# Which queue carries the third and fourth block of x at the start of a one-core kernel

## The chip, the cores and the metric

The kernel runs on one core of one Trainium2 chip. Times are device microseconds of one execution. Before the change three runs were timed: 234.91 us is their median, 234.7 and 235.87 us the ends. A separate execution was recorded by the hardware profiler; all rows of the profile come from that one.

## The reference

The input A_q (2048 tokens, 640 wide, bf16) is normalised per token; the result xn feeds two branches, and both are added to A_q. Cut to what matters:

```python
x = A_q
xn = _layernorm(x, axis=-1)
# branch A: a 4-tap shift of k, times v, a causal convolution of length 2048 per channel
# (by Fourier transforms), plus kv * ssm_D, times xn
# branch B:
g = jnp.einsum("bsd,df->bsf", xn, w_gate)          # 640 -> 1728
u = jnp.einsum("bsd,df->bsf", xn, w_up)
h = _sigmoid(g) * u
B = jnp.einsum("bsf,fd->bsd", h, w_down)           # 1728 -> 640
return x + A + B
```

## The kernel before, in words

The 2048 tokens lie as 16 blocks: token 16 p + b is partition p of block b, so one block is a tile of 128 x 640, 160 KB, whose rows are 1280 bytes each. Four blocks make a token tile t of 512 tokens. Branch B runs tile by tile: for each of 14 chunks of 128 hidden columns a gate product and an up product of five matmuls each (the 640 channels are five chunks of 128), the sigmoid on ScalarE (L300), the product of both on VectorE (L306), then the down products. Branch A works on five chunks of 128 channels, with matmuls against Fourier tables, evictions by ScalarE and VectorE, and round trips through DRAM. The long middle of the kernel is a list of steps whose order over all engines is written out by hand (ORDER); each engine works its own instructions in that order. Nearly all transfers are issued from SyncE, in the order of that list; SyncE's queue is q1 in the profile, ScalarE's is q10. 

The change is at the front, ahead of the list, where the first token tile is got ready block by block:

- x blocks 0 and 1 are loaded in halves of 320 columns, one half from SyncE and one from ScalarE (L515).
- x blocks 2 and 3 are loaded whole (L517), one from each queue.
- Gate and up columns 0 to 255 (load_w, L184 and L187; 320 KB each, in rows of 512 bytes) follow on SyncE, then columns 256 to 511, then the transfers of the list.
- For each block, VectorE takes the statistics (bn_stats, L213, two per block; L217, L241), GpSimd the power -1/2 (L245), and VectorE writes the normalised block xn (L250). On VectorE these stand in the order: statistics of 0, statistics of 1, xn of 0, statistics of 2, xn of 1, statistics of 3, xn of 2, xn of 3, with the small steps between.
- TensorE turns each xn block by five transposes (turn, L264), ScalarE copies the result to xnT (L267).
- TensorE then works the string FIRST: gate and up products of the first two hidden chunks in quarters of 128 tokens (quarter, L282), "g01" being gate, chunk 0, block 1, and "t2" the turn of block 2:

```python
FIRST = """
g00 g10 t1 u00 u10 t2 g01 g11 u01 u11 t3 g02 u02 g12 u12 g03 u03 g13 u13
"""
```

Block 0 is turned before that. Ahead of the real products TensorE runs matmuls on zeros (busy, L528). ScalarE's first work is one small activation with its table load (L130).

Of the kernel before, what the change touches and what calls it, by code (L numbers as in the profile page):

```python
# [65 lines left out]
def kernel(  # L66
# [14 lines left out]
    nc = tc.nc  # L81
    xr = A_q.flatten_outer_dims().rearrange("(p b) d -> p b d", b=NB)
# [33 lines left out]
    x = res.tile([P, NB, DM], BF16, name="x")  # L116
# [15 lines left out]
    sync = nc.sync  # L132
# [381 lines left out]
        for i in range(2):  # L514
            (sync, nc.scalar)[i].dma_start(x[:, b, 320 * i:320 * i + 320], xr[:, b, 320 * i:320 * i + 320])  # L515
    for i in range(2):
        (sync, nc.scalar)[i].dma_start(x[:, 2 + i, :], xr[:, 2 + i, :])  # L517
    for u in range(2):
        load_w(sync, 0, 256, u)
    for u in range(2):  # L520
# [210 lines left out]
```

## Time and profile before

| what | value |
|---|---|
| three timed runs | 234.7, 234.91, 235.87 us |
| the profiled execution | 235.94 us |
| its span, first to last instruction | 234.2 us |
| TensorE busy | 227.0 us, 97% of the span |
| VectorE busy | 204.1 us, 87% |
| ScalarE busy | 131.5 us, 56% |
| DMA q1 (SyncE) | 55.35 MB, 88.2% of 16 engines |
| DMA q10 (ScalarE) | 0.36 MB, 0.5% |
| granted TensorE clock | full throughout |

Times in the rows are microseconds from the start of the span. A row of the timeline has the start, the duration, the engine (SPq and ACTq are the queues' issues by SyncE and ScalarE, PEld the weight loads of TensorE), the line, the operation, what is written and read, the number of instructions and, in brackets, the idle time before it and what ended it. The duration of an issue is the time that it takes to hand the transfer over, not the time of the transfer. DMA engines' busy share can be over 1 where packets overlap.

### The profile page before, as it was taken

The numbers are of one execution on the slowest core, as the hardware profiler recorded it, in microseconds if no ns is written. First come the engines' busy times: TensorE is split into PE (matmuls) and PEld (weight loads), VectorE is DVE, ScalarE is ACT, GpSimd is POOL, SyncE is SP. The second block draws the span as 40 slices with busy tenths as digits, with TensorE's granted clock in tenths as the row PEclk, the third lists the DMA queues.
The fourth block names the chain that finished last, engine by engine and source line by source line (L and its number), as shares of the span: only waits on it lengthen the run. The fifth ranks groups of instructions, "written<-read, shape, count | busy, mean of one in ns | idle before, by whom it ended". The sixth has DMA issues, their size and how long they took to land.

```text
span 234.2 us, 5584 instructions
## 1 busy us (share of the span) xinstructions
PE 227.0 (97%) x2270; PEld 112.8 (48%) x2281; DVE 204.1 (87%) x323; ACT 131.5 (56%) x191; POOL 12.7 (5%) x27
## 2 busy tenths in 40 slices
PE   7799999999999999999999999999999999999993
PEld 2664444447444444446444444445563545445582
DVE  5532789999969999999999999999999999999574
ACT  2347832438985877866647666855555776652000
POOL 5201200000020000012001000000000000000000
PEclk9999999999999999999999999999999999999999
DMA  6999999799789987978879998999989769784775
GB/s 176 278 305 235 246 344 203 208 243 304 198 270 293 317 213 211 249 164 243 212 261 266 309 272 214 271 227 258 321 200 247 213 180 255 182 217 145 216 266 148
DMA packets 98143, 56.07 MB, mean 239 GB/s; under 512 B 56326, under 2 KB 92358, under 8 KB 97990
## 3 DMA queue, kind: packets, MB, share of 16 engines
q1 hardware_dynamic: 97542, 55.35, 88.2%
q10 hardware_dynamic: 576, 0.36, 0.5%
q8 instruction: 18, 0.29, 0.5%
q14 instruction: 7, 0.06, 0.1%
HBM read 35.39 MB, written 18.35 MB: 229 GB/s over the span
## 4 chain that ended last, share of the span: by engine, by line
PE 79%; DVE 12%; DMA 4%; issue 2%; SPq 1%; ACT 1%; DVEq 0%
PE pg L291 22%; PE pu L291 22%; PE pd L329 14%; PE psb L500 3%; PE pr L340 3%; PE ps L400 3%; PE ps L398 3%; DMA w<-in_B_w_up_dram 3%; PE ps L432 3%; PE psa L461 2%; DVE tmp L377 2%; PE pg L312 1%; DVE acc L379 1%; DVE yx L505 1%; DMA SMt<-tabSM 1%
## 5 line engine op out<-in xcount | busy, mean ns | idle before, releaser
L291 PEld LDWEIGHTS <-w 128*128 128x128 bf16 x500 | 47.1, 98 | 57.4 <-issue 4.0
L291 PE MATMUL pu<-xnT,w 128*128 128x512 bf16 x250 | 62.2, 379 | 0.0
L291 PE MATMUL pg<-xnT,w 128*128 128x512 bf16 x250 | 62.2, 379 | 0.0
L329 PE MATMUL pd<-wd,hT 128*128 128x512 bf16 x213 | 50.4, 379 | 0.7 <-issue 0.2
L306 DVE TENSOR_TENSOR hT<-sig,pu 128x512 bf16<-128x512 bf16 x52 | 34.6, 679 | 12.8 <-ACT sig L300 6.9
L254 ACT CAST t<-ps 128x1024 bf16<-128x1024 f32 x33 | 32.3, 1013 | 21.9 <-PE ps L400 21.9
L300 ACT ACTIVATE sig<-pg 128x512 bf16<-128x512 f32 x52 | 30.6, 598 | 23.7 <-PE pg L291 20.1
L254 ACT CAST xz<-ps 128x1024 bf16<-128x1024 f32 x30 | 29.5, 1015 | 14.3 <-PE ps L432 14.3
L329 PEld LDWEIGHTS <-hT 128*128 128x128 bf16 x224 | 21.3, 98 | 25.1 <-issue 0.9
L447 DVE TENSOR_TENSOR xz<-xz 128x2048 bf16<-128x2048 bf16 x20 | 24.4, 1218 | 0.3
L377 DVE TENSOR_TENSOR tmp<-kx,sc 128x1024 bf16<-128x1024 bf16 x30 | 20.9, 698 | 0.4
L379 DVE TENSOR_TENSOR acc<-acc,tmp 128x1024 bf16<-128x1024 bf16 x30 | 20.6, 685 | 0.5
L505 DVE TENSOR_TENSOR yx<-psb,xn 128x512 bf16<-128x512 f32 x20 | 13.8, 688 | 2.6 <-PE psb L500 1.8
L400 PE MATMUL ps<-kvh,S1t 128*128 128x512 bf16 x40 | 15.5, 387 | 0.0
L254 ACT CAST ao<-psa 128x1024 bf16<-128x1024 f32 x11 | 10.8, 1014 | 8.3 <-PE psa L461 8.2
L398 PE MATMUL ps<-kvh,S1t 128*128 128x512 bf16 x40 | 15.1, 379 | 0.0
L445 DVE STREAM_SHUFFLE xz<-xz 128x512 f32<-128x512 f32 x20 | 14.5, 725 | 0.0
L340 PE MATMUL pr<-wd,hT 128*128 128x128 bf16 x224 | 13.8, 219 | 0.0
L340 PEld LDWEIGHTS <-hT 128*128 128x128 bf16 x224 | 13.0, 98 | 1.8 <-issue 0.6
L334 DVE TENSOR_TENSOR x<-pd,x 128x512 bf16<-128x512 f32 x16 | 10.7, 684 | 2.1 <-PE pd L329 2.0
L257 DVE CAST xz<-ps 128x1024 bf16<-128x1024 f32 x10 | 12.1, 1215 | 0.4 <-PE ps L432 0.4
L500 PEld LDWEIGHTS <-TBt 128*128 128x128 bf16 x160 | 9.7, 98 | 3.4 <-issue 1.5
(57 smaller groups left out, 183.9 us busy)
## 6 DMA issues: line engine op xcount, KB each, us to landing
d<-t SPq DMA_DIRECT2D x20, 512.0 KB, 5.1
t<-d SPq DMA_DIRECT2D x20, 512.0 KB, 5.5
bi<-d SPq DMA_DIRECT2D x8, 512.0 KB, 5.3
d<-ao SPq DMA_DIRECT2D x6, 512.0 KB, 5.7
kvh<-in_A_v_dram SPq DMA_DIRECT2D x10, 256.0 KB, 5.3
kx<-in_A_k_dram SPq DMA_DIRECT2D x10, 256.0 KB, 4.6
hn<-in_A_ssm_k_dram SPq DMA_DIRECT2D x20, 128.0 KB, 4.6
x<-in_A_q_dram SPq DMA_DIRECT2D x3, 640.0 KB, 5.1
```

Source lines behind the costliest of these rows:

```text
L254: nc.scalar.copy(out=out, in_=in_)
L291: nc.tensor.matmul(pg[:, :], lhsT=w[:, c, u * UP + fc * P:u * UP + (fc + 1) * P], rhs=xnT[:, :, c, :], start=(c == 0), stop=(c == NC - 1))
L300: nc.scalar.activation(sig[fc][:, :], pgs[0, fc][:, :], ACT.Sigmoid)
L306: nc.vector.tensor_tensor(hT[:, fc, :], sig[fc][:, :], pgs[1, fc][:, :], ALU.mult)
L329: nc.tensor.matmul(pds[bb][:, :], lhsT=hT[:, fc, bb * P:(bb + 1) * P], rhs=wd[:, fc, 0:4 * P], start=(fc == 0), stop=(fc == NFC - 1))
L340: nc.tensor.matmul(pds[t, b0][:, bb, :], lhsT=hT[:, fc, bb * P:(bb + 1) * P], rhs=wd[:, fc, 4 * P:DM], start=(fc == 0), stop=(fc == NFC - 1))
L377: nc.vector.tensor_tensor(d["tmp"][:, :, :], kx[:, lo + 3 - m:hi + 3 - m, :], sb(m), ALU.mult)
L379: nc.vector.tensor_tensor(d["acc"][:, :, :], d["acc"][:, :, :], d["tmp"][:, :, :], ALU.add)
L398: nc.tensor.matmul(ps[:, 0, :, :], lhsT=S1[:, h, :], rhs=cin[c]["kvh"][:, 0, 4 * n4:4 * n4 + 4, :], start=True, stop=True)
L400: nc.tensor.matmul(ps[:, 1, :, :], lhsT=S1[:, h, :], rhs=hp[:, 2 * n4:2 * n4 + 2, :, :], start=True, stop=True)
L447: nc.vector.tensor_tensor(z[:, 1:3, :, :], z[:, 0:1, :, :].to_broadcast((P, 2, 8, P)), z[:, 1:3, :, :], ALU.mult)
L500: nc.tensor.matmul(ps[:, i, :], lhsT=TB[:, h, 4 * m + i, :], rhs=bi[:, h, 4 * (m % 2) + i, :], start=(h == 0), stop=(h == 1))
```

## The change

Both whole blocks of x are issued from ScalarE, block 2 first and block 3 behind it, after ScalarE's halves of blocks 0 and 1. SyncE's queue thereby holds its halves of blocks 0 and 1 and directly behind them the first gate and up columns. The number, size and program order of the transfers stay the same.

```diff
     for i in range(2):
-        (sync, nc.scalar)[i].dma_start(x[:, 2 + i, :], xr[:, 2 + i, :])
+        nc.scalar.dma_start(x[:, 2 + i, :], xr[:, 2 + i, :])
     for u in range(2):
         load_w(sync, 0, 256, u)
     for u in range(2):
         load_w(sync, 256, 512, u)
```

## The prediction

> **What bounds the kernel now.** I read the page's busy times first, then the table of engine busy time by stretch, then the chain of waits for the first 14 us, and last the timeline and the DMA view of those microseconds. The table by stretch tells where lost time can be:
>
> ```profile
> core 0: us, PE busy (x) PEld busy (x) DVE busy (x) ACT busy (x) POOL busy (x), PEclk, DMA share, GB/s
> 0.00:8.10 8.10, 5.61 (x18) 1.95 (x18) 5.01 (x17) 2.18 (x3) 4.02 (x14) 1.00 0.77 210
> 9.30:36.00 26.70, 26.70 (x184) 14.52 (x185) 13.84 (x21) 15.20 (x31) 2.64 (x5) 1.00 1.06 279
> 90.00:120.00 30.00, 29.63 (x295) 14.59 (x296) 29.49 (x45) 21.63 (x32) 2.96 (x3) 1.00 0.88 223
> ```
>
> From 9.3 us on, TensorE is busy for all of 26.70 us, and even in the stretch where VectorE is fullest (29.49 of 30.00 us) it loses 0.37 us. So the time at which TensorE's real work gets going decides the end, and a change at the front is worth at most the shift of that point. The chain says what sets the point:
>
> ```profile
> 1.65 0.42 SPq L517
> 2.07 0.04 issue
> 2.12 0.43 SPq L184
> 2.55 0.04 issue
> 2.59 6.63 DMA w<-in_B_w_up_dram
> 9.22 0.05 issue
> 9.27 0.73 PE pu L282 x10
> ```
>
> The chain goes through SyncE's issue of x block 2 (L517), the first gate columns (L184) and the first up columns, waits 6.63 us until those up columns have landed at 9.22 us, and continues on TensorE. The edit takes the L517 link of 0.42 us out of exactly this chain, so it looks like a gain. The question is whether 6.63 us is counted from the issue (then all of it moves) or ends when the bytes ahead have gone through (then nothing moves).
>
> **Part 1: SyncE's queue loses one issue.** The issues as they stand:
>
> ```profile
> 1.16 1.28 ACT L130 ACT_TABLE_LOAD   x1 [1.16 <-PEq L715]
> 1.65 0.42 SPq L517 DMA_DIRECT2D x<-in_A_q_dram  x1
> 1.65 0.45 ACTq L517 DMA_DIRECT2D x<-in_A_q_dram  x1
> 2.12 0.43 SPq L184 DMA_DIRECT2D w<-in_B_w_gate_dram  x1
> 2.59 0.53 SPq L187 DMA_DIRECT2D w<-in_B_w_up_dram  x1
> 3.22 0.94 SPq L184 DMA_DIRECT2D w<-in_B_w_gate_dram  x1
> 4.20 1.50 SPq L187 DMA_DIRECT2D w<-in_B_w_up_dram  x1
> 5.74 3.03 SPq L184 DMA_DIRECT2D w<-in_B_w_gate_dram  x2
> ```
>
> Without block 2 the gate columns are issued at 1.65 instead of 2.12 us: 0.47 us earlier, and the up columns as well. The transfers behind them gain less: the third and fourth weight transfers take 0.94 and 1.50 us to issue, and the next two 3.03 us together, where a free issue takes 0.43 us. From 3.22 us on SyncE is held up by transfers that are still queued, so its head start runs out there; nothing later comes sooner by it unless the engines have moved more by then. Whether they have is read from the transfer side:
>
> ```profile
> 2.00:3.00 1.00, 1.00 (x4) 0.44 (x3) 0.01 (x1) 0.65 (x2) 1.00 (x3) 1.00 0.97 285
> 3.00:4.00 1.00, 1.00 (x4) 0.32 (x3) 0.97 (x3) 0.00 (x0) 0.04 (x1) 1.00 0.88 166
> 4.00:5.00 1.00, 1.00 (x4) 0.30 (x2) 0.96 (x4) 0.00 (x0) 0.53 (x1) 1.00 0.85 287
> 5.00:6.00 1.00, 1.00 (x8) 0.43 (x7) 0.79 (x4) 0.00 (x0) 0.13 (x2) 1.00 1.07 320
> 6.00:7.00 1.00, 0.79 (x6) 0.18 (x3) 0.94 (x3) 0.69 (x1) 0.47 (x1) 1.00 1.12 306
> ```
>
> The last two columns are the DMA engines' busy share and rate, one row for each microsecond. From 2 us on the 16 engines are never empty: 0.97, 0.88, 0.85, then over 1. All that must land before the up products is the same before and after: four blocks of x and two weight transfers, 4 x 160 + 2 x 320 = 1280 KB, in another order. An earlier issue can only fill what is unfilled: 0.03 + 0.12 + 0.15 = 0.30 us of the three first rows. That is the upper end of the ordinary gain. I take 0, because the unfilled part is in the rows after 3 us, when weights issued at 2.12 and 2.59 us stood in the queue already: the engines were slow there, not short of work. The row 3 to 4 us is the odd one, 166 GB/s at 88% busy; it comes back as a rival.
>
> **Part 2: ScalarE's queue gains one issue.** Block 3 is issued behind block 2, at 1.65 + 0.45 + 0.05 = 2.15 instead of 1.65 us, and one more issue of 0.45 us stands on ScalarE. Behind it is only the warm-up activation; the table load (1.16 us, 1.28 us long) already runs beside the issue at 1.65 us, and ScalarE's first product copy is far behind:
>
> ```profile
> 6.18 0.69 ACT L267 COPY xnT<-pt 128x640 bf16<-128x640 bf16 x1 [3.52 <-PE pt L264]
> ```
>
> It had been idle for 3.52 us. Cost 0; if that cover were gone it would be 0.45 us.
>
> **Part 3: when blocks 2 and 3 land.** Which queue gets how much of the engines is seen where both hold work. The two queues' rows for 2 to 3 us (both hold 640-byte rows of x), and after them for 5.5 to 6 us:
>
> ```profile
> q1 hardware_dynamic: 258, 0.15, 51.1%
> q10 hardware_dynamic: 236, 0.14, 45.6%
> ...
> q1 hardware_dynamic: 315, 0.16, 106.3%
> q10 hardware_dynamic: 3, 0.00, 1.5%
> ```
>
> q1 is SyncE's, q10 ScalarE's: 258 packets against 236, turn by turn. In 5.5 to 6 us ScalarE's queue starts its last three, so block 3 ends there, about when block 2 does. Now each of block 2's 128 rows takes its turn with one 512-byte weight row instead of a 1280-byte row of block 3: 128 x 768 = 98 KB less ahead of its end, 0.3 us at 306 GB/s. Block 3 follows, with 256 weight rows let through before its end: 131 KB, 0.43 us later. Who waits for them:
>
> ```profile
> 5.67 0.15 DVE L241 TENSOR_SCALAR lnq<-mv 128x1 f32<-128x1 f32 x1
> 6.05 0.89 DVE L213 BATCH_NORM_STATS2 st<-x 128x6 f32<-128x320 bf16 x2 [0.23 <-DMA x<-in_A_q_dram]
> 7.51 0.88 DVE L213 BATCH_NORM_STATS2 st<-x 128x6 f32<-128x320 bf16 x2
> 8.30 0.43 DVE L250 TENSOR_SCALAR xn<-x,mv,lnq 128x640 bf16<-128x640 bf16 x1
> 9.71 0.45 DVE L250 TENSOR_SCALAR xn<-x,mv,lnq 128x640 bf16<-128x640 bf16 x1 [0.67 <-POOL lnq L245]
> 8.13 0.73 PE L282 MATMUL pg<-xnT,w 128*128 128x128 bf16 x10 [1.34 <-DMA w<-in_B_w_gate_dram]
> 9.78 0.32 PEld L264 LDWEIGHTS <-xn 128*128 128x128 bf16 x5
> 11.18 0.32 PEld L264 LDWEIGHTS <-xn 128*128 128x128 bf16 x5
> ```
>
> The statistics of block 2 waited 0.23 us for it, until 6.05 us; this wait goes, and VectorE is free at 5.82. Block 3's statistics start at 7.51 us without a wait, or 7.28 once the 0.23 are gone. Block 3 then lands some 0.43 us after its old end, near 6.5 to 6.8 us: still in time. And what is gained here ends in slack: xn of block 2 is ready at 8.30 + 0.43 = 8.73 and its turning starts at 9.78 (1.05 us later); xn of block 3 is ready at 10.16 and turned at 11.18 (1.02 us later). TensorE reaches these turns only after the weight waits, so neither a small gain nor a small loss in x moves the end.
>
> **Sum.** 0 (part 1, bounds -0.30 and 0) + 0 (part 2) + 0 (part 3). Against the profiled execution, 235.94 us with a span of 234.2, that is 235.9; its 1.74 us outside the span are untouched. That execution lay 1.03 us above the median of the three timed runs (234.91; 234.7 to 235.87), so the forecast for the median is **234.9 us**, and 0.5%, about what a measurement of this kernel can tell from no change, is 1.17 us.
>
> At part 3 one rule speaks against the change. The Trainium skill, page "DMA: Bandwidth & Descriptors", section "Queues, rings and completion order", says that a DMA engine takes a whole packet from one queue, typically 9 to 17 descriptors and up to 64, before it turns to the other. With 64 weight rows for each engine ahead of block 2, 64 x 16 x 512 bytes = 524 KB, block 2 would, as an estimate from that page and the 306 GB/s, land 1.7 us later, at 7.76; by the slack above that adds 7.76 - 7.07 = 0.7 us, 235.6 instead of 234.9. The trace cannot show it: where two queues met, both carried x.
>
> **The rivals.**
>
> *A. ScalarE's queue gets the smaller share (slower).* Now the long weight transfers compete with x from the first moment, where they came behind half of it. Block 2's statistics stand at the head of VectorE's line; behind them are xn of block 1 and everything of blocks 2 and 3. The deciding point is block 2 landing at 6.05 + 1.02 = 7.07 us; every microsecond beyond is one on the end. If it lands only with the gate columns (TensorE's start at 8.13) the price is 1.06 us: 236.0. If only with the up columns (9.22) it is 2.15 us: 237.1. For it: 512-byte weight rows stand in long lines of 640 KB against 320 KB of x. Against it: the 258 to 236 above. Chance 0.19.
>
> *B. The slow microsecond goes, or the laggard catches up (faster).* In 3 to 4 us, just when 1280-byte rows of x went through both queues, the rate was 166 instead of 287 GB/s. If it is that pairing, the edit ends it: (287 - 166) / 287 = 0.42 us earlier, 234.5. And the transfers are uneven over the engines; for 0 to 9.2 us the DMA view has
>
> ```profile
> q1 hardware_dynamic: 3110, 1.67, 68.2%
> ```
>
> SyncE's queue owed 0.98 MB by then (320 KB of x, 640 KB of weights); it had moved 1.67, so 0.69 MB of later transfers, some two of them, were through before the last part of the up columns. At 9.22 - 8.13 = 1.1 us for a transfer, an even spread would bring the up columns some 2 us sooner, of which the turns' slack lets 1.02 + 0.23 = 1.25 us through: 233.7. For it: nothing but that the order at the very spot changes. Against it: no row ties the lag to the order, and the three timed runs already differ by 1.2 us. Chance 0.23 in all, 0.15 of it near the end of 233.7 or below.
>
> *C. The change does not do what it says.* SyncE's issue could be held at the second weight transfer already, so the weights' order hardly moves. No time changes: 234.9. Chance 0.06; the forecast itself has 0.52.
>
> **How the numbers follow.** The forecast and C lie within 0.5%, as do B's lower part (0.08): 0.66. Faster by over 0.5% is B's far end, 0.15; slower is A, 0.19, whose price of 1.06 to 2.15 us begins just short of the 1.17. The likeliest case's own range is 234.3 to 235.9 (0.3 + 0.3 below for the idle share and the runs' spread, 1.0 above as the runs show). To leave out no more than 2 in 10, the range reaches to B's bound and half-way into A: 233.6 to 236.6.
>
> **What would show it.** In the changed profile, SyncE's gate issue at about 1.65 us, two issues from L517 on ScalarE at about 1.65 and 2.15; the third weight issue again near 3.2 us; no wait before block 2's statistics and none before block 3's; TensorE's first gate products near 8.1 us and up products near 9.2 to 9.3. Wrong would be: up products before 8.6 us (then B), a wait for x of over 1 us before the statistics of block 2 or 3 together with a gap before a turn of L264 (then A), or a shift of the end that is not there at 9.3 us, which would mean that the front does not decide alone.

## The result, and the profile after

The changed kernel takes **236.54 us** (median of six runs, 236.29 to 236.60) against 234.89 for the kernel before (six runs, 234.7 to 235.87): 1.0061 times as long, with a 95% interval of 1.0048 to 1.0075, or about 1.4 us; the two medians lie 1.65 us apart. The forecast was 234.9. Its profiled execution took 236.49 us, with a span of 234.6.

The chain of waits of the changed kernel for the first 14 us (start, duration, what):

```profile
0.72 2.52 DMA x<-in_A_q_dram
3.24 0.02 issue
3.26 5.63 DMA x<-in_A_q_dram
8.88 0.02 issue
8.91 0.89 DVE st L213 x2
9.79 0.36 DVE xn L250
10.15 0.05 issue
10.20 0.45 PE pt L264 x5
```

The up columns are gone from the chain. In their place stands x, twice: a transfer of x that ends at 3.24 us, another that is issued at 3.26 and lands at 8.88, and then the statistics that waited for it. The timeline of the issues shows which one it is:

```profile
1.65 0.43 SPq L184 DMA_DIRECT2D w<-in_B_w_gate_dram  x1
1.65 0.45 ACTq L517 DMA_DIRECT2D x<-in_A_q_dram  x1
2.12 0.53 SPq L187 DMA_DIRECT2D w<-in_B_w_up_dram  x1
2.69 0.53 SPq L184 DMA_DIRECT2D w<-in_B_w_gate_dram  x1
3.26 0.52 SPq L187 DMA_DIRECT2D w<-in_B_w_up_dram  x1
3.26 0.40 ACTq L517 DMA_DIRECT2D x<-in_A_q_dram  x1
```

Block 2 leaves ScalarE at 1.65 us. Block 3 does not follow at 2.15, but at 3.26, behind three of SyncE's weight transfers and beside the fourth. The program says why. The framework that builds it gives the transfers of both queues eight semaphores in turn (counters by which an engine learns that a transfer has landed), and a ninth must wait until the first has landed. ScalarE's first instructions:

```
L515 DMACopy x<-in_A_q_dram 128x320
L130 LoadActFuncSet
L130 Activation warm<-mhalf 128x4 [waits Pool_49]
L515 DMACopy x<-in_A_q_dram 128x320
L517 DMACopy x<-in_A_q_dram 128x640
L517 DMACopy x<-in_A_q_dram 128x640 [waits DMAHW0_49]
```

The last of them waits for the first semaphore, which belongs to ScalarE's half of block 0. That half landed at 3.24 us, and the issue begins 0.02 us later. The same 0.02 us of issue stand in the chain of each of the five profiled executions in which block 3 is ninth (the changed kernel and four versions below), at 3.16 to 3.31 us. In the order in which the semaphores are handed out the second gate columns are now the eighth transfer and block 3 is the ninth; before, it was the second gate columns that stood ninth.

VectorE's statistics and xn of blocks 2 and 3 and TensorE's start of each step, in the changed kernel:

```profile
6.58 0.89 DVE L213 BATCH_NORM_STATS2 st<-x 128x6 f32<-128x320 bf16 x2 [0.69 <-DMA x<-in_A_q_dram]
8.91 0.89 DVE L213 BATCH_NORM_STATS2 st<-x 128x6 f32<-128x320 bf16 x2 [0.79 <-DMA x<-in_A_q_dram]
9.71 0.43 DVE L250 TENSOR_SCALAR xn<-x,mv,lnq 128x640 bf16<-128x640 bf16 x1
11.11 0.45 DVE L250 TENSOR_SCALAR xn<-x,mv,lnq 128x640 bf16<-128x640 bf16 x1 [0.67 <-POOL lnq L245]
6.87 0.72 PE L282 MATMUL pg<-xnT,w 128*128 128x128 bf16 x10
10.20 0.28 PEld L264 LDWEIGHTS <-xn 128*128 128x128 bf16 x5 [1.49 <-DVE xn L250]
11.62 0.45 PE L264 MATMUL pt<-ident,xn 128*128 128x128 bf16 x5
14.15 0.81 PE L291 MATMUL pg<-xnT,w 128*128 128x512 bf16 x3
```

The gate products do begin early, at 6.87 us, but TensorE's weight loads then stand idle for 1.49 us (its matmuls for 1.32) ahead of block 2's turn, and its dense stage (L291) begins at 14.15 us. In the prediction's execution of the kernel before that stage began at 13.75, only 0.4 us sooner; that execution, at 235.94 us, was itself one of the longest of its kernel. So the kernel before was profiled once more.

### The profile page after: what moved, and what is told of

Same layout as the page of the kernel before. It is cut to its first block, busy times and chain, and to the rows that moved or that the text cites. A ratio compares the mean times of both kernels' runs of the same rounds, so it can differ in the third digit from the quotient of the medians.

```text
span 234.6 us, 5595 instructions
## 1 busy us (share of the span) xinstructions
PE 227.7 (97%) x2281; PEld 112.7 (48%) x2281; DVE 204.3 (87%) x323; ACT 131.5 (56%) x191; POOL 12.7 (5%) x27
## 4 chain that ended last, share of the span: by engine, by line
PE 80%; DVE 13%; DMA 3%; issue 1%; DVEq 0%
PE pg L291 22%; PE pu L291 22%; PE pd L329 14%; PE psb L500 3%; DMA x<-in_A_q_dram 3%; PE pr L340 3%; PE ps L400 3%; PE ps L398 3%; PE ps L432 3%; PE psa L461 2%; DVE tmp L377 2%; DVE xz L257 1%; PE pg L312 1%; DVE acc L379 1%; DVE yx L505 1%
## 5 line engine op out<-in xcount | busy, mean ns | idle before, releaser
L291 PEld LDWEIGHTS <-w 128*128 128x128 bf16 x500 | 47.0, 97 | 57.4 <-issue 4.0
L291 PE MATMUL pu<-xnT,w 128*128 128x512 bf16 x250 | 62.2, 379 | 0.0
L291 PE MATMUL pg<-xnT,w 128*128 128x512 bf16 x250 | 62.2, 379 | 0.0
L329 PE MATMUL pd<-wd,hT 128*128 128x512 bf16 x224 | 51.5, 379 | 0.0
```

Source lines behind the costliest of these rows:

```text
L291: nc.tensor.matmul(pg[:, :], lhsT=w[:, c, u * UP + fc * P:u * UP + (fc + 1) * P], rhs=xnT[:, :, c, :], start=(c == 0), stop=(c == NC - 1))
L329: nc.tensor.matmul(pds[bb][:, :], lhsT=hT[:, fc, bb * P:(bb + 1) * P], rhs=wd[:, fc, 0:4 * P], start=(fc == 0), stop=(fc == NFC - 1))
```

## The experiments

Two theories stood against each other. **W**: block 3 is late because its issue waits for a semaphore, and so gets behind SyncE's weights. **S** (the prediction's rival A): ScalarE's queue has too small a share of the DMA engines, whenever it is issued.

**The kernel before, once more.** No edit.

> The kernel before, profiled once more; nothing is changed. The first profiled execution took 235.94 us, 1.05 over the median of six. Theory: the spread of the kernel before is the landing of the first up columns on the slowest DMA engine; an execution at 234.7 to 234.9 us starts its up products near 8.2 us instead of 9.27, and everything behind is the same. Rival: the up products start at 9.2 to 9.3 us again and the microsecond is lost elsewhere.

It took 234.85 us, span 233.0. Its rows for the same steps:

```profile
5.84 0.88 DVE L213 BATCH_NORM_STATS2 st<-x 128x6 f32<-128x320 bf16 x2
7.29 0.88 DVE L213 BATCH_NORM_STATS2 st<-x 128x6 f32<-128x320 bf16 x2
8.08 0.43 DVE L250 TENSOR_SCALAR xn<-x,mv,lnq 128x640 bf16<-128x640 bf16 x1
9.48 0.45 DVE L250 TENSOR_SCALAR xn<-x,mv,lnq 128x640 bf16<-128x640 bf16 x1 [0.66 <-POOL lnq L245]
7.02 0.73 PE L282 MATMUL pg<-xnT,w 128*128 128x128 bf16 x10
8.15 0.73 PE L282 MATMUL pu<-xnT,w 128*128 128x128 bf16 x10
8.71 0.44 PE L264 MATMUL pt<-ident,xn 128*128 128x128 bf16 x5
10.11 0.44 PE L264 MATMUL pt<-ident,xn 128*128 128x128 bf16 x5
12.63 1.24 PE L291 MATMUL pg<-xnT,w 128*128 128x512 bf16 x5
```

As the theory said: the up products start at 8.15 instead of 9.27 us, the dense stage at 12.63. Two things follow. From the dense stage to the end of the span are 233.0 - 12.63 = 220.4 us here, 234.2 - 13.75 = 220.4 in the first execution and 234.6 - 14.15 = 220.4 in the changed kernel, so everything is decided in front of it, and 14.15 - 12.63 = 1.52 us is the loss. And the slack is small: block 2 is ready at 8.08 + 0.43 = 8.51 and turned at 8.71, block 3 at 9.93 and turned at 10.11. Weights and x come just in time for each other; the 1.05 and 1.02 us of slack in the prediction belonged to an execution whose weights were late.

**Block 1 whole** (one transfer fewer, so that no semaphore has to be waited for):

```diff
-    for b in range(2):
-        for i in range(2):
-            (sync, nc.scalar)[i].dma_start(x[:, b, 320 * i:320 * i + 320], xr[:, b, 320 * i:320 * i + 320])
+    for i in range(2):
+        (sync, nc.scalar)[i].dma_start(x[:, 0, 320 * i:320 * i + 320], xr[:, 0, 320 * i:320 * i + 320])
+    sync.dma_start(x[:, 1, :], xr[:, 1, :])
```

> The changed kernel with block 1 loaded whole from SyncE instead of in halves: one transfer fewer ahead, so that block 3 is not the ninth and its issue on ScalarE has no semaphore to wait for. Theory W (the late issue is the cause): block 3 is issued near 2.1 us instead of 3.26, lands before 7.5 us, statistics of block 3 wait less than 0.3 us, first gate products near 6.9 us stay, and the time is 233.7 to 235.0 us, at or below the kernel before. Rival S (ScalarE's queue has too small a share of the DMA engines whenever it is issued): block 3 lands after 8 us again and the time is 236.0 to 236.8 us.

234.89 us (ten runs) against 235.00 for the kernel before beside it: ratio 0.9995, interval 0.9986 to 1.0004. Block 2 and block 3 are issued together from ScalarE and block 3's statistics start at 7.41 us without a wait:

```profile
1.21 0.87 ACTq L517 DMA_DIRECT2D x<-in_A_q_dram  x2
5.97 0.88 DVE L213 BATCH_NORM_STATS2 st<-x 128x6 f32<-128x320 bf16 x2
7.41 0.88 DVE L213 BATCH_NORM_STATS2 st<-x 128x6 f32<-128x320 bf16 x2
12.72 1.24 PE L291 MATMUL pg<-xnT,w 128*128 128x512 bf16 x5
```

As W expected, though the gate products started at 7.30 and not 6.87 us. Both blocks of x go through ScalarE's queue, block 3 beside the weights, and the loss is gone: S falls. But the edit also moves block 1 and lets ScalarE issue both blocks 0.44 us sooner than in the changed kernel, so the wait alone is not yet isolated.

**Blocks 2 and 3 as one transfer:**

```diff
-    for i in range(2):
-        nc.scalar.dma_start(x[:, 2 + i, :], xr[:, 2 + i, :])
+    nc.scalar.dma_start(x[:, 2:4, :], xr[:, 2:4, :])
```

> The changed kernel with blocks 2 and 3 in one transfer on ScalarE (320 KB, rows of 2560 bytes), issued third in its queue, near 1.65 us, without a semaphore to wait for. Theory W: both blocks land together by 6.8 us; block 2's statistics wait a little longer than the 0.69 us now, block 3's not at all; time 233.9 to 235.2 us. Rival S: the transfer lands after 8 us, then block 2 is late as well and the time is over 237 us.

235.74 us, ratio 1.0037 (1.0025 to 1.0050). The blocks landed together at 6.54 us, as W said and S did not; the time is above W's range (233.9 to 235.2). Block 2's statistics wait 0.76 us for the whole transfer, and with the little slack just seen the dense stage starts at 13.24.

```profile
6.56 0.89 DVE L213 BATCH_NORM_STATS2 st<-x 128x6 f32<-128x320 bf16 x2 [0.76 <-DMA x<-in_A_q_dram]
```

**SyncE held until block 3 has landed** (a 16-byte store of it; one transfer of weights fewer ahead of block 3, so no semaphore wait):

```diff
     for u in range(2):
         load_w(sync, 0, 256, u)
+    hold = dr.tile([1, 8], BF16, name="hold")
+    sync.dma_start(hold[:, :], x[0:1, 3, 0:8])
```

> The changed kernel with a 16-byte store of block 3 on SyncE behind the first gate and up columns: SyncE issues nothing more until block 3 has landed. It also makes block 3 the eighth transfer, without a semaphore to wait for. Theory W: block 3 is issued near 2.1 us, its first packets move about 1 us later, it lands before 7 us and VectorE does not wait for it over 0.3 us. Rival S: the first two weight transfers alone crowd ScalarE's queue and block 3 lands after 7.5 us.

Block 3 was issued at 2.14 us and landed at 7.21, and VectorE did not wait for it; W had said before 7, S after 7.5, so it lies between them. Block 2 landed at 6.52, so that the dense stage began at 13.24. The rest of the loss at 236.51 us has another source: 234.7 - 13.24 = 221.5 us for the rest instead of 220.4, since all later weights are held.

**SyncE held until block 1 has landed.** This takes the semaphore wait away. The later weights are issued at 4.12 and 4.55 us, 0.3 to 0.9 us after those of the kernel before; all else is the changed kernel:

```diff
     for u in range(2):
         load_w(sync, 0, 256, u)
+    hold = dr.tile([1, 8], BF16, name="hold")
+    sync.dma_start(hold[:, :], x[0:1, 1, 320:328])
```

> The changed kernel with a 16-byte store of block 1 on SyncE behind the first gate and up columns: SyncE issues its next weights only when ScalarE's half of block 1 has landed, near 3.7 us, about when the kernel before issued them (3.3 and 3.7), and block 3 becomes the eighth transfer, without a semaphore to wait for. All else is as in the changed kernel. Theory W: block 3 issued at 2.1 us, landed by 7.3, block 2 still near 6.5 us as its rows share the engines with the first weights; main products start near 13.2 instead of 14.15 us; time 235.4 to 235.9 us. So of the loss of 1.5 us some 0.9 is the semaphore wait and 0.6 the sharing. Rival S: block 3 after 8 us, 236.4 us or more.

```profile
1.66 1.01 ACTq L517 DMA_DIRECT2D x<-in_A_q_dram  x2
5.87 0.88 DVE L213 BATCH_NORM_STATS2 st<-x 128x6 f32<-128x320 bf16 x2
7.32 0.88 DVE L213 BATCH_NORM_STATS2 st<-x 128x6 f32<-128x320 bf16 x2
12.57 1.24 PE L291 MATMUL pg<-xnT,w 128*128 128x512 bf16 x5
```

235.18 us (ten runs) against 235.04, ratio 1.0012 (0.9999 to 1.0025): nearly all of the loss is gone, more than W expected, and the dense stage starts at 12.57. The 0.6 us that I had put down to sharing was not there, because block 2 landed at 5.68 us. Over the twelve executions profiled here block 2 landed anywhere from 5.1 to 6.7 us (4.2 with block 1 whole), with no clear tie to the order of the weights. This spread has a price of its own: where block 2 landed after 6.5 us but block 3 was not late (one transfer, held until block 3, and the next version) the dense stage began at 13.24 to 13.45 us.

**Half of the change**: block 2 on ScalarE, block 3 on SyncE behind the first gate and up columns.

```diff
-    for i in range(2):
-        nc.scalar.dma_start(x[:, 2 + i, :], xr[:, 2 + i, :])
+    nc.scalar.dma_start(x[:, 2, :], xr[:, 2, :])
     for u in range(2):
         load_w(sync, 0, 256, u)
+    sync.dma_start(x[:, 3, :], xr[:, 3, :])
```

> Half of the change: block 2 on ScalarE, but block 3 on SyncE behind the first gate and up columns, in one ring with them, with no semaphore to wait for. By the order of the ring block 3 lands 0.5 to 0.6 us after the up columns (7.5 to 8.0 us in the other runs): 8.0 to 8.6 us. With VectorE's statistics of block 3 the point that decides, main products start 5.25 us after them, at 13.4 to 13.9 us; time 235.7 to 236.3 us. Rival: if TensorE's weights decide instead, main products start by 12.9 us and the time is 235.2 us or less.

Up columns landed at 7.71, block 3 at 8.18 us, the dense stage began at 13.45, the time was 235.76 us: all as expected, but not by the expected step.

```profile
6.76 0.89 DVE L213 BATCH_NORM_STATS2 st<-x 128x6 f32<-128x320 bf16 x2 [0.83 <-DMA x<-in_A_q_dram]
8.21 0.88 DVE L213 BATCH_NORM_STATS2 st<-x 128x6 f32<-128x320 bf16 x2
```

VectorE waited 0.83 us for block 2, which landed only at 6.74 us, and when it came to block 3 that was just there. The chain of waits of this execution goes through block 2 as well, so the dense stage's 0.8 us are block 2's. That block 3 alone would cost as much behind the first weights, 8.18 us against the 7.29 at which the kernel before starts its statistics, is an estimate.

**VectorE's order**, to see which step behind the late block decides:

```diff
-    ln_stats(0, 3)
     ln_xn(0, 2)
+    ln_stats(0, 3)
     ln_ready(0, 3)
```

> The changed kernel with one exchange in VectorE's order: xn of block 2 ahead of the statistics of block 3, so that block 2's turn no longer stands behind the late block. Theory (the chain through block 3 itself decides, block 2 behind it only fills): block 2 is turned near 9.0 instead of 10.20 us, block 3 at 11.6 us as before, main products at 14.1 us, time 236.3 to 236.6 us. Rival (block 2's turn behind the statistics is the loss): main products at 13.2 us or less, time 235.7 us.

236.46 us. Block 2 was turned at 9.11 instead of 10.20 us, block 3 at 11.71, the dense stage began at 14.24. The 1.49 us of idle time in the changed kernel's row for block 2's turn is thus not the price by itself: the chain from block 3's landing over its own statistics and xn to its turn is.

**What a late issue costs.** In the changed kernel block 3's issue had ended at 3.66 us and its first packet moved only at 7.01. Three kernels keep the semaphore wait (issue at 3.2 to 3.3 us) and hold SyncE until block 3 has landed, with one, two or three weight transfers issued ahead of it. Small loads of 16 bytes keep block 3 ninth. The one with two ahead:

```diff
+    pre = res.tile([1, 8], BF16, name="pre")
+    sync.dma_start(pre[:, :], xr[0:1, 0, 0:8])
...
     for u in range(2):
         load_w(sync, 0, 256, u)
+    hold = dr.tile([1, 8], BF16, name="hold")
+    sync.dma_start(hold[:, :], x[0:1, 3, 0:8])
```

> The changed kernel with SyncE held until block 3 has landed, and one 16-byte load more ahead, so that block 3 is the ninth transfer again and waits for the same semaphore: it is issued near 3.26 us as in the changed kernel, but no weights beyond the first gate and up columns have been issued by then. In the changed kernel its first packet moved at 7.01 us, 3.4 us after the issue had ended at 3.66. Theory H (its descriptors were made only after those of SyncE's later weights, which had no room): first packets of block 3 right behind block 2's, without a gap of over 0.5 us, block 3 landed by 7.3 us. Rival (a late issue on ScalarE's queue costs it its turn, whatever SyncE has issued): a gap again, first packets after 6.5 us, landed after 8.

With one ahead, the store stands behind the first gate columns and there are two small loads; with three it stands behind the second gate columns and there is none:

> As hold_late (block 3 issued near 3.2 us after the semaphore wait, SyncE held until it has landed), but with only the first gate columns issued ahead; two 16-byte loads keep block 3 the ninth transfer or later. The first packet of block 3 moved at 5.78 us with two weight transfers ahead and at 7.01 in the changed kernel. Theory H (block 3's descriptors come after those of the weights issued before it, and these wait for room as the engines drain): with one ahead the first packet moves near 4.3 us, right behind block 2's, and block 3 lands by 6.5 us. Rival (a fixed delay of a late issue): 5.8 us again, landed at 7.9. The up columns are late here by design, so the time itself tells nothing.

> The changed kernel with SyncE held behind three weight transfers (first gate, first up, second gate) until block 3 has landed; block 3 waits for the same semaphore and is issued near 3.2 us. Theory H: with the three issued ahead of it and nothing behind them the first packet of block 3 moves near 7.0 us and it lands near 8.9, as in the changed kernel, since the fourth weight transfer was issued together with it or later. Rival (the fourth transfer or the mere sharing of the engines makes it late): first packet near 5.8 us, landed by 8 us.

ScalarE's queue (q10) in the DMA view, with one transfer ahead: 5 to 5.7 us, with SyncE's (q1) beside it, then 5.7 to 6.5.

```profile
q10 hardware_dynamic: 118, 0.14, 53.8%
q1 hardware_dynamic: 154, 0.07, 35.2%
...
q10 hardware_dynamic: 22, 0.02, 7.8%
```

With two ahead, the same stretches, then 6.5 to 7 and 7 to 8 us:

```profile
q10 hardware_dynamic: 1, 0.00, 0.1%
...
q10 hardware_dynamic: 85, 0.10, 42.2%
...
q10 hardware_dynamic: 50, 0.05, 36.3%
...
q10 hardware_dynamic: 9, 0.01, 2.6%
```

With three ahead there is nothing of q10 from 5.7 to 7 us; the rows are 6.5 to 7 us, where only SyncE's queue stands, and 7 to 8, where both do:

```profile
q1 hardware_dynamic: 294, 0.15, 115.5%
...
q10 hardware_dynamic: 129, 0.15, 52.0%
q1 hardware_dynamic: 241, 0.12, 46.1%
```

| weight transfers ahead | block 3 issued | its first packet | landed |
|---|---|---|---|
| 1 | 3.33 us | 4.95 us | 6.63 us |
| 2 | 3.18 | 5.78 | 7.88 |
| 3 | 3.31 | 7.01 | 8.95 |
| changed kernel (the fourth issued beside it) | 3.26 | 7.01 | 8.88 |

From one transfer ahead to two and to three, each 320 KB transfer that SyncE had issued ahead puts block 3 back by 0.8 to 1.3 us (first packet and landing), about the 1.1 us that one takes, although block 3 is in the other queue; the fourth, issued at the same moment, does nothing. So when block 3 starts is set by the order of issue, not by a share. It does not wait for the last transfer ahead to end, though: its first packet moved when 469 of 640 weight rows ahead of it had started (one transfer), 992 of 1280 (two) and 1660 of 1920 (three), and from there on the two queues interleave, as the rows show. With one ahead most of the wait is not SyncE's: the last packet of block 2, in block 3's own queue, started at 4.71 us. Each row of the table is one execution. The expectation for two ahead failed in its numbers (a gap of 0.8 us where none over 0.5 was expected, 7.88 instead of 7.3 us): I had counted only the weights beyond the first pair, but the pair itself holds block 3 back. The first packet with one ahead was 0.65 us later than expected; with three ahead both figures came as expected. In time, with two ahead the dense stage starts at 13.15 and with three at 14.21: of the 1.52 us some 0.5 is the wait with the first pair ahead and 1.0 the second gate columns that the wait let by. Of these three kernels only the stretch up to there is read, since SyncE is held and the whole takes 237.05 to 237.41 us.

## Why the prediction was wrong

**The step that failed is part 2.** It put block 3's issue at 2.15 us, after the 0.45 us of the issue before it, and counted as cost only ScalarE's work behind it. The issue itself waited until 3.24 us for a semaphore, +1.1 us. The kernel before had a trace of that: its third weight issue begins at 3.22 us, 0.10 after the one before it had ended instead of the usual 0.04, and it was that transfer which stood ninth. I read the row as an engine held up by transfers in its queue and never counted the semaphores.

**Part 3 then missed the landing.** Block 3 was to land 0.43 us later, near 6.5 to 6.8. It landed at 8.88, against 6.05 in the second execution before: +2.83. Most of that is the late start: no packet of block 3 moved for 3.3 us after its issue had ended. The turn-by-turn sharing was mis-sized besides. The 258 against 236 packets were x against x; in the changed kernel block 2 met the weights, and from 4.5 to 5 us the queues moved

```profile
q1 hardware_dynamic: 197, 0.10, 66.0%
q10 hardware_dynamic: 73, 0.08, 44.5%
```

While block 2's 128 rows moved (3.64 to 5.61 us), 741 weight rows went by, not 128. So the gain of 0.3 us for block 2 is not to be seen; it landed at 6.56, in a spread larger than that. And even when issued at 2.14 us, block 3 landed at 7.19 and 7.21 us (the holds until block 1 and until block 3), later than the 6.5 to 6.8 of the prediction though still in time for VectorE. The prediction's remark that the trace could not show such a meeting was wrong: in the kernel before, weights and the end of block 3 were on the move together from 4.5 to 5 us (218 packets against 27).

**The slack was mis-sized.** 1.02 us came from one execution 1.05 above its kernel's median. In the other one it is 0.18. With that, statistics of block 3 at 8.91 instead of 7.29 us (+1.62, less 0.18) give about 1.44 us on the end, near the 1.52 of the traces and the 1.65 between the medians. The profiled execution and the median differed by 0.4%, and I carried the difference into the time but not into the slack.

**Part 1** was right at its ends: gate columns issued at 1.65 us and no gain in the end from it. It was wrong between. The third weight issue came at 2.69 us, not near 3.2, as it no longer stood ninth. That head start is what put a third transfer ahead of block 3.

**The rivals.** A had the right sign and engine: VectorE's line stood behind a late block of x, and its price of 1.06 to 2.15 us holds the measured one. The late block was 3, not 2, and a smaller share was not the cause of the loss: with block 1 whole and with the hold until block 1 both blocks still go through ScalarE's queue, in the second both beside weights, and the loss is gone or nearly so (0.9995 and 1.0012 times the kernel before). That the range ended at 236.6, 0.06 us above the measured 236.54, is therefore luck: it owes that end to A's price, not to the mechanism that the runs showed. The rule weighed at part 3 (the Trainium skill, page "DMA: Bandwidth & Descriptors", section "Queues, rings and completion order"), that an engine drains a whole packet before it turns to the other queue, would have had block 2 at 7.76 us by its ceiling; it landed at 6.56, which speaks against the ceiling here but not against smaller packets. B's early weights came in part (gate products at 6.87 us, up products at 8.16, which the prediction had named as B's sign), and were worth nothing: with x in time (block 1 whole, or the hold until block 1) the time is that of the kernel before. The chain of waits then holds no weights; with block 1 whole it runs from block 0's landing at 3.19 us through its statistics, xn and turn to the gate products at 7.30, and xn of block 3 is ready at 10.06 for a turn at 10.19. B's slow microsecond, 3 to 4 us, did not go, and the pairing of two queues with 1280-byte rows is not its cause. In the changed kernel only ScalarE's queue has such rows there, with block 1 whole both queues do:

```profile
3.00:4.00 1.00, 1.00 (x4) 0.31 (x3) 0.91 (x3) 0.00 (x0) 0.04 (x1) 1.00 0.60 80
3.00:4.00 1.00, 1.00 (x4) 0.31 (x3) 0.79 (x2) 0.00 (x0) 0.04 (x1) 1.00 1.02 308
```

The changed kernel moved 80 GB/s in it and block 1 whole 308. No version that was run beats the kernel before. What C feared is not to be seen: the first three weight issues follow each other at 1.65, 2.12 and 2.69 us.

What stays open is where block 3's packets wait. That its rows are handed to the DMA engines only once SyncE's earlier ones have found room would give this order, but no row shows this handing over.

## What to carry to other kernels

Before moving a transfer to another queue, list all transfers of both queues in the order in which semaphores are handed out: moving one can make a critical transfer the one that reuses a semaphore and so has to wait for a landing. A small transfer that is needed soon must be issued ahead of bulk transfers even if these are on the other queue. And read slack from an execution near the median, or from two.

## What the runs showed that was not expected

A transfer issued on ScalarE's queue did not start to move until most of the bulk that SyncE had issued before it was under way: with one, two and three transfers of 320 KB ahead its first packet moved 1.6, 2.6 and 3.7 us after its issue began (with one ahead, block 2 in the same queue explains most of it). The Trainium skill, page "DMA: Bandwidth & Descriptors", section "Issuing engines are not separate DMA queues", says that transfers of all queues interleave on the same 16 engines and that a second issuing engine saves only issue time. For packets that are on the move the trace agrees (block 2 beside the weights, 73 packets to 197 from 4.5 to 5 us). But when the first packet of a transfer moves was decided by the order of issue across both queues.
